# Routing attention and a squared-ReLU FFN on one core: 20 instead of 16 weight blocks rounded in the first half of batch 0, 12 instead of 16 in the second

## The chip, the core and the metric

The kernel runs on one NeuronCore of a Trainium2 chip. The core has five engines, each with its own instruction queue that it works through in order: PE (TensorE, matrix products), DVE (VectorE), ACT (ScalarE), POOL (GpSimd) and SP (SyncE, which here issues DMAs). They run side by side and wait for one another by semaphores. SBUF is the on-chip memory with 128 partitions, PSUM holds the products of PE. The metric is the device time of one execution in microseconds (us); the time before is the median of 15 executions.

## The reference

Inputs: q, k, v of shape (batch 4, heads 8, sequence 768, head width 64), 16 centroids per head, and two weight matrices of 512x2048 and 2048x512, all float32.

```
q_assign = argmax(norm(q) @ norm(centroids).T)          # cluster of each query
k_assign = argmax(norm(k) @ norm(centroids).T)          # cluster of each key
scores   = (q @ k.T) / sqrt(64), -1e9 where the clusters differ
attn     = softmax(scores)
x        = (attn @ v), heads side by side -> (3072, 512)
out      = relu(x @ w_in)**2 @ w_out                    # (3072, 512)
```

## The kernel before

**Units.** The eight heads are taken in four pairs per batch, the 768 queries in two halves of 384, the 768 keys in six chunks of 128. A unit is one pair, one half of the queries and two chunks of keys: three units make a pair's half. Batch 0 has 24 units. Units 0 to 11 are the first half of the queries for pairs 0 to 3, units 12 to 23 the second half; `TWOS`, which is 12, marks the border (L731). Batches 1 to 3 follow pair by pair.

**One unit.** `scores` (L447) makes the products `sc` on PE, in batch 0 a float32 part from `qkT` and a bfloat16 part from `ohT` that sets pairs of different clusters far below the others. ACT takes their exponential (`exp`, L474) into `ex`. Two units later in units 0 to 11, and one or two later from unit 12 on, `times_v` (L505) multiplies by v (`av`). The softmax sums are made in one of two ways: for the first half of batch 0 by PE products with a constant (`sm`, inside `times_v`), otherwise by POOL additions into `acc` (L488, L490) and one short product at the end. `add_up` (L531) takes the reciprocal `r` of the sums on DVE (L545), sends it through DRAM and back over the partitions (`far_r`, `rb`, L548 and L551, by SP), and `finish` (L561) multiplies it into `xT` on DVE (L564). PSUM has two buffers for scores (`ps_sc`), two for `av` and `sm`, and two (`ps_f`) that transposes, logits and FFN products share.

**Preparing the next pair.** In batch 0 the items of `prep` (L416) for the next pair are spread over a pair's three units: three groups of transposes `pt` (L259) with ACT copies into `qkT` (L263), the logits `lg` and their ACT copy `lgs` (L312), the transposes `lt` of these (L322), five DVE steps that find the cluster number, from `mx` (L345) through L346, L349 and L352 to the one-hot rows `oh` (L354), the transposes `po` of `oh` (L389) and two ACT copies into `ohT` (L397, L399). The next pair's scores need `qkT` and `ohT`. From batch 1 on the route goes by DRAM (`words`, `flat`, `qid`).

**The FFN of batch 0** is made in small steps between the units from unit 12 on (`ffn`, L573: products `ph`, then `po` at L591). It starts when `xT` of pair 3's first half is there. The other batches' FFNs run at the end, after all attention, in a form with seven products in place of eight (`ffn_pair`, L604).

**The weights.** The two matrices are cut into 32 blocks of 128 x 512, sixteen of `w_in` and then sixteen of `w_out`, here called blocks 0 to 31. They reach SBUF as 64-bit words, so a block's load is 128 x 1024 32-bit words (512 KB), into one of four buffers (`wstage`, `AHEAD` = 4). `round_weights` (L141) turns a block into the form that the products use: two ACT steps (L150, L152), three DVE steps (L155, L159, L163) and one POOL step (L167). Then `load_weights` issues the load of the fourth next block on SP (L139), which waits until POOL has ended with the block whose buffer it takes.

**What sets the order.** A planner in the framework orders the instructions of each engine from the program's order, the priorities (`tc.high_priority`) and explicit constraints (`tc.issue_after`). The rounding steps of a unit may come only after the last `exp` that was written before them:

```
rounding += 4
while rounding >= 3:
    rounding -= 3
    i = next(to_round, None)
    if i is not None:
        with tc.issue_after(last_exp[0]):
            round_weights(i)
```

Four is added per unit and three taken per block, so the units take 1, 1, 2, 1, 1, 2, ... blocks, and unit 23 takes the last.

Of the kernel before, what the change touches and what calls it, by code (L numbers as in the profile page):

```python
# [25 lines left out]
def kernel(  # L26
# [88 lines left out]
    def load_v(pair):  # L115
        b, hp = divmod(pair, HP)
        raw_v[pair] = loads_v.tile([P, 2, NCH, D], F32, name="v_raw")
        nc.sync.dma_start(
            raw_v[pair], v[b, 2 * hp : 2 * hp + 2].rearrange("h (p j) d -> p h j d", p=P)
        )  # L120
# [16 lines left out]
    def load_weights(i):  # L137
        raw_w[i] = wstage.tile([P, NW, 2], U32, name="w_raw")
        nc.sync.dma_start(raw_w[i], weights[i][1])  # L139
# [134 lines left out]
    def split_words(pair, which):  # L274
        if which == 0:
            words[pair] = dram.tile([2 * NCH, P, 2, 2 * D], U16, name="words")
        flat = loads.tile([P, NCH, 2, 2 * D], U16, name="flat", tag="qk")
        src = raw[pair][which].bitcast(U16).rearrange("p c (d two) -> p c two d", two=2)
        half = NCH // 2
        with tc.issue_after(last_exp[0]):  # L280
            for cols in (slice(0, half), slice(half, NCH)):
                nc.scalar.copy(out=flat[:, cols], in_=src[:, cols])
        nc.sync.dma_start(
            words[pair][NCH * which : NCH * (which + 1)].rearrange("c p two d -> p c two d"),
            flat,
        )
        if which == 1:
            raw.pop(pair)
            load_qk(pair + 1)
# [126 lines left out]
    def prep(pair):  # L416
        if pair < HP:
            return [
                lambda: turn(pair, 0), lambda: turn(pair, 1), lambda: turn(pair, 2),
                lambda: logits(pair), lambda: route(pair),  # L420
                lambda: turn_onehot(pair, 0), lambda: turn_onehot(pair, 1),
            ]

        split = [lambda i=i: split_words(pair + 1, i) for i in range(2 if pair + 1 < NG else 0)]
        first, second = split or (None, None)
        return [
            lambda: turn_words(pair), None, None, first, None, None,
            lambda: logits(pair), None, lambda: route(pair), second, None, None,
            None, None, lambda: spread(pair),
        ]  # L430
# [10 lines left out]
    def first_half(pair, h):  # L441
        return pair < HP and h == 0
# [62 lines left out]
    def times_v(pair, h, c):  # L505
        if c == 0:
            av[pair, h] = ps_av.tile([P, TB], F32, name="av", tag="av")
            if first_half(pair, h):
                sums[pair, h] = ps_av.tile([P, TB // 2], F32, name="sm", tag="av")
        t = ex.pop((pair, h, c))  # L510
        products = [
            dict(
                out=av[pair, h][D * e : D * (e + 1)], lhsT=raw_v[pair][:, e, c + i],
                rhs=t[:, 2 * i + e], start=(c + i == 0), stop=(c + i == NCH - 1),
            )
            for i in range(2) for e in range(2)
        ]
        if first_half(pair, h):
            for i in range(2):
                one = [  # L520
                    ones_products(
                        sums[pair, h], e, t[:, 2 * i + e], c + i == 0, c + i == NCH - 1
                    )
                    for e in range(2)
                ]
                products += [p for both in zip(*one) for p in both]
        together(products, 4000)
# [3 lines left out]
    def add_up(pair, h):  # L531


        b, hp = divmod(pair, HP)
        if first_half(pair, h):
            sm = sums.pop((pair, h))
            nc.scalar.copy(out=xT_of(b, h)[:, hp], in_=av.pop((pair, h)))
        else:
            total = acc.pop((pair, h))
            sm = bank("sm", [P, TB // 2])  # L540
            one = [ones_products(sm, e, total[:, e], True, True) for e in range(2)]
            together([p for both in zip(*one) for p in both])
        row = 4 * (2 * pair + h)
        r = once.tile([P, TB // 2], F32, name="r")
        nc.vector.reciprocal(out=r, in_=sm)  # L545
        r = r.rearrange("(r p) n -> r p n", r=4)[:, 0]
        far = dram.tile([2, TB], F32, name="far_r")
        nc.sync.dma_start(far.rearrange("e (g n) -> (e g) n", g=2), r)  # L548
        rb = rbp.tile([P, TB], F32, name="rb")
        for e in range(2):  # L550
            nc.sync.dma_start(rb[D * e : D * (e + 1)], far[e].partition_broadcast(D))  # L551
        nc.sync.dma_start(seen[row : row + 4], r)
        spread_out[pair, h] = rb
# [177 lines left out]
    TWOS = HP * NCH // 2  # L731
# [17 lines left out]
    def behind_first(u, what=last_logits):  # L749
        return tc.issue_after(what[0]) if u == 0 else ExitStack()  # L750

    def next_pair(u):

        pair, h, c = units[u]
        if c == 0 and pair + 1 < NG and h == 0 and (pair + 1) not in qkT:
            if pair + 1 < HP or pair >= HP:
                return pair + 1
        if u == TWOS + 4:
            return HP
        return None  # L760
# [10 lines left out]
    rounding = 0  # L771
# [6 lines left out]
    def ends(halves):  # L778
        for pair, h in halves:
            b, hp = divmod(pair, HP)  # L780

            with tc.high_priority(offset=1000) if (pair, h) == (HP - 1, 0) else ExitStack():
                finish(pair, h)
            if hp == HP - 1 and (b, h) in PLAIN:
                fill.append(ffn(b, h))

    for u in range(len(units) + 3):
        if u < len(units):
            pair, h, c = units[u]
            if (p := next_pair(u)) is not None:  # L790
                ahead.extend(prep(p))
            if u in (TWOS, TWOS + 2):

                split_words(HP, int(u > TWOS))
            if c == 0 and u + 3 < len(units) and units[u + 3][0] not in raw_v:
                load_v(units[u + 3][0])

            with behind_first(u):
                scores(pair, h, c)

        ends(added)
        added.clear()
        if u < TWOS:
            ready = u - 1
        elif u == TWOS or u % 2 or u >= len(units):
            ready = u

        complete, late = late, []
        while v_next < min(ready, len(units)):
            pair, h, c = units[v_next]  # L810
            times_v(pair, h, c)
            v_next += 1
            if c == NCH - 2:
                (late if h and not HP * NCH <= u < len(units) else complete).append((pair, h))
        for pair, h in complete:
            with tc.high_priority(offset=1000) if first_half(pair, h) else ExitStack():
                add_up(pair, h)
            if h == 1:
                for d in (qkT, ids, qid):
                    d.pop(pair)  # L820
            if h == 1 or pair < HP:
                raw_v.pop(pair)
            added.append((pair, h))

        rounding += 4
        while rounding >= 3:
            rounding -= 3
            i = next(to_round, None)
# [3 lines that stand above are left out]
                if (i := next(loaded, None)) is not None:  # L832
                    load_weights(i)
            elif not later:
                early.close()
                for name, bufs in (("xT", 5), ("out", 2)):
                    later[name] = keep.enter_context(
                        tc.tile_pool(name=name + "_late", bufs=bufs, side="right",
                                     reuse_waits="tile")
                    )  # L840
        share = 0
        if u % 2 == 0 or not TWOS < u < len(units):
            n = 2 if TWOS < u < len(units) else 1
            share = max(0, left[0] - RESERVE) * sum(map(density, range(u, u + n)))
            share //= max(1, sum(map(density, range(u, ENDS))))
        goal = left[0] - share

        for i in range(3):
            if i == 2:
                fill_steps(share * 2 // 3)  # L850
            if ahead:
                with behind_first(u, masked if i else last_logits):
                    (ahead.pop(0) or int)()
        fill_steps(left[0] - goal)
# [235 lines left out]
```

## Time and profile before

| | us |
|---|---|
| median of 15 executions | 979.13 (976.9 to 984.9) |
| the profiled execution | 983.98 |
| its span, first to last instruction | 982.2 |
| PE busy | 962.1 (98%) |
| DVE busy | 565.5 (58%) |
| POOL busy | 380.6 (39%) |
| ACT busy | 316.3 (32%) |
| exp of unit 0 starts | 19.11 |
| exp of unit 12 starts | 77.61 |
| FFN products of batch 0 run through from | 88.77 |
| the last FFNs (L670, L701) start | 542.2 |

Times inside the span are counted from its first instruction. "Busy" counts the time in which an instruction of the engine is under way; matrix products are pipelined, so a busy PE need not be a PE at its peak. "x <- y" in a row of waits or in brackets behind an instruction says what ended the idle time before it. The starts of exp in units 1 to 14 are 22.94, 27.59, 33.78, 38.06, 43.64, 49.76, 54.04, 59.63, 65.75, 69.00, 72.26, 77.61, 82.15 and 86.14.

### The profile page before, as it was taken

Reading aid. Unit: us, or ns where it says so; the run is one execution under the profiler, and the core shown is the slowest. Engines: PE = TensorE matmul, PEld = TensorE weight load, DVE = VectorE, ACT = ScalarE, POOL = GpSimd, SP = SyncE. Lnnn points to the kernel's source line nnn. Section 1 sums busy time; section 2 is a strip of 40 time slices with the busy share of each in tenths; the row PEclk is TensorE's granted clock in tenths of the full one; section 3 lists DMA queues with packets and bytes.
Section 4 is the critical chain, followed back from the end, with each engine's and each line's share of the span. In section 5 each row is a group of like instructions: output and inputs, shape, how many; then the busy total and the mean of one; then the engine's idle time right before and its main releaser. Section 6 shows DMA issues by size and latency. Waiting matters only on the chain.

```text
span 982.2 us, 12064 instructions
## 1 busy us (share of the span) xinstructions
PE 962.1 (98%) x4479; PEld 553.2 (56%) x4479; DVE 565.5 (58%) x913; ACT 316.3 (32%) x511; POOL 380.6 (39%) x277
## 2 busy tenths in 40 slices
PE   8999999999999999999999999999999999999997
PEld 5444444443344444444443555888556888556886
DVE  4779766665666656566657865532566531656331
ACT  4787755443435554454331111000111000111000
POOL 1237865556565565555656431002231002231000
PEclk9999999999999999999999999999999999999999
DMA  9657681455544445443310000000000000000000
GB/s 239 193 166 217 192 195 61 111 117 129 133 114 118 121 121 122 113 119 89 88 36 17 20 1 0 12 22 22 11 1 1 22 22 22 1 1 0 22 22 25
DMA packets 127746, 74.54 MB, mean 76 GB/s; under 512 B 90944, under 2 KB 119104, under 8 KB 127680
## 3 DMA queue, kind: packets, MB, share of 16 engines
q1 hardware_dynamic: 125968, 73.26, 28.2%
q8 instruction: 38, 0.62, 0.3%
q10 hardware_dynamic: 1712, 0.43, 0.2%
q14 instruction: 28, 0.23, 0.1%
HBM read 48.27 MB, written 15.86 MB: 65 GB/s over the span
## 4 chain that ended last, share of the span: by engine, by line
PE 85%; issue 5%; POOL 3%; DMA 2%; DVE 2%; SPq 1%; ACT 0%; POOLq 0%; DVEq 0%; ACTq 0%
PE bank L701 22%; PE bank L670 22%; PE po L591 8%; PE ph L578 7%; PE sc L91 6%; PE sc L94 6%; PE av L91 5%; PE av L94 5%; POOL w_in L167 2%; PE sm L91 1%; PE lg L91 1%; DMA rb<-far_r 1%; DMA qid<-far 1%; DVE ex L478 1%; SPq L109 1%
## 5 line engine op out<-in xcount | busy, mean ns | idle before, releaser
L490 POOL TENSOR_TENSOR acc<-acc,ex 128x768 f32<-128x768 f32 x112 | 206.8, 1846 | 109.5 <-DVE ex L478 93.1
L478 DVE SCALAR_TENSOR_TENSOR ex<-qid,ids,sc 128x384 f32<-128x384 bf16 x288 | 157.9, 609 | 65.7 <-ACT sc L474 41.9
L474 ACT ACTIVATE sc<-sc 128x768 f32<-128x768 f32 x144 | 108.5, 793 | 160.5 <-PE sc L94 142.7
L94 PE MATMUL sc<-qkT 64*128 64x384 f32 x576 | 153.6, 507 | 0.5
L94 PE MATMUL av<-ex,v_raw 128*64 128x384 f32 x576 | 136.9, 495 | 0.0
L659 POOL TENSOR_TENSOR w_s<-w_in 128x256 f32<-128x256 f32 x24 | 18.1, 756 | 273.9 <-PE bank L701 162.0
L640 DVE TENSOR_TENSOR g<-bank,g 128x384 f32<-128x384 f32 x144 | 77.8, 555 | 79.1 <-PE bank L670 77.9
L578 PE MATMUL ph<-xT,w_in 128*128 128x384 f32 x256 | 91.8, 499 | 4.8 <-DVE best L346 2.2
L701 PE MATMUL bank<-w_out,g 128*128 128x256 f32 x432 | 95.2, 379 | 0.0
L591 PE MATMUL po<-w_out,gT 128*128 128x512 f32 x192 | 91.7, 609 | 0.0
L91 PE MATMUL sc<-qkT 64*128 64x384 f32 x192 | 88.0, 539 | 3.2 <-DVE ex L478 3.2
L701 PEld LDWEIGHTS bank<-w_out,g 128*128 128x128 f32 x432 | 82.1, 190 | 11.8
L640 DVE TENSOR_TENSOR osb<-bank,osb 128x256 f32<-128x256 f32 x54 | 22.1, 423 | 107.6 <-PE bank L701 102.2
L94 PEld LDWEIGHTS sc<-qkT 64*128 64x128 f32 x576 | 65.5, 187 | 28.0 <-issue 5.7
L91 PE MATMUL av<-ex,v_raw 128*64 128x384 f32 x192 | 81.1, 504 | 0.0
L488 POOL TENSOR_TENSOR acc<-ex 128x768 f32<-128x768 f32 x28 | 51.5, 1840 | 52.4 <-DVE ex L478 42.3
L578 PEld LDWEIGHTS ph<-xT,w_in 128*128 128x128 f32 x256 | 45.7, 189 | 43.8 <-issue 14.1
L670 PE MATMUL bank<-xT,w_in 128*128 128x384 f32 x192 | 69.9, 487 | 0.0
L670 PE MATMUL bank<-x_t,w_s 128*128 128x384 f32 x192 | 69.8, 486 | 0.0
L670 PE MATMUL bank<-xT,w_s 128*128 128x384 f32 x192 | 69.8, 486 | 0.0
L94 PEld LDWEIGHTS av<-ex,v_raw 128*64 128x64 f32 x576 | 49.7, 137 | 34.7 <-issue 34.4
L701 PE MATMUL bank<-w_t,g 128*128 128x256 f32 x288 | 65.1, 379 | 0.0
(127 smaller groups left out, 1228.3 us busy)
## 6 DMA issues: line engine op xcount, KB each, us to landing
words<-flat SPq DMA_DIRECT2D x24, 384.0 KB
w_raw<-in_moe_w_in_dram SPq DMA_DIRECT2D x16, 512.0 KB
w_raw<-in_moe_w_out_dram SPq DMA_DIRECT2D x16, 512.0 KB
v_raw<-in_v_dram SPq DMA_DIRECT2D x20, 384.0 KB
rb<-far_r SPq DMA_DIRECT2D x64, 96.0 KB
q_raw<-in_q_dram SPq DMA_DIRECT2D x31, 192.0 KB
k_raw<-in_k_dram SPq DMA_DIRECT2D x31, 192.0 KB
out_dram<-osb SPq DMA_DIRECT2D x23, 256.0 KB
```

The lines of the kernel that those rows point to most:

```text
L91: last = nc.tensor.matmul(**next(products))
L94: last = nc.tensor.matmul(**product)
L167: nc.gpsimd.tensor_tensor(out=dst, in0=dst, in1=lo, op=ALU.add)
L474: last_exp[0] = nc.scalar.activation(out=t[:, 2 * i : 2 * i + 2] if pair < HP else src, in_=src, func=ACT.Exp, scale=SCALE).ins
L478: last_mask[0] = nc.vector.scalar_tensor_tensor(out=t[:, 2 * i + e], in0=qid[pair][1][:, h, e], scalar=ids[pair][:, ch % NB, 2 + ch // NB, ...
L488: nc.gpsimd.tensor_tensor(out=acc[pair, h], in0=t[:, 0:2], in1=t[:, 2:4], op=ALU.add)
L490: nc.gpsimd.tensor_tensor(out=acc[pair, h], in0=acc[pair, h], in1=t[:, 2 * i : 2 * i + 2], op=ALU.add)
L578: nc.tensor.matmul(ph, lhsT=w_in[:, kk, f * P : (f + 1) * P], rhs=xT[b, h][:, kk], start=(kk == 0), stop=(kk == KT - 1),)
L591: nc.tensor.matmul(po, lhsT=gT[f][:, i * P : (i + 1) * P], rhs=w_out[:, f], start=(f == 0), stop=(f == FT - 1),)
L640: nc.vector.tensor_tensor(out=out, in0=bank, in1=to, op=ALU.add)
L670: nc.tensor.matmul(bank, lhsT=operands[j][0][:, kk], rhs=operands[j][1][:, kk], start=(kk == 0), stop=(kk == H2 - 1),)
L701: nc.tensor.matmul(bank, lhsT=operands[j][0][:, f], rhs=operands[j][1][:, f], start=(f == 0), stop=(f == F2 - 1),)
```

## The change

Per unit five is added in units 0 to 11 and three in units 12 to 23, in place of four in both; three are taken per block as before.

```diff
-        rounding += 4
+        rounding += 5 if u < TWOS else 3
         while rounding >= 3:
             rounding -= 3
             i = next(to_round, None)
```

Units 0 to 11 now take 1, 2, 2, 1, 2, 2, ... blocks, 20 in all: all of `w_in` and four blocks of `w_out`. Units 12 to 23 take one each. The steps of a block, its buffers and the number of blocks stay as they are; as a block's load is issued behind the rounding of the fourth block before it, the loads move with the rounding. The planner then orders a few other instructions differently in units 1 to 8: the transposes `lt` stand behind all eight float32 score products of their unit in place of four (in unit 2 also behind three of the four mask products), and in unit 3 the scores stand ahead of `po` and `av` behind it.

## The prediction

> **What bounds the kernel now.** I read the page's engine lines first, then the stages, then PE's waits in each stage, then the timelines of the chains that PE waits for.
>
> ```profile
> PE 962.1 (98%) x4479; PEld 553.2 (56%) x4479; DVE 565.5 (58%) x913; ACT 316.3 (32%) x511; POOL 380.6 (39%) x277
> ```
>
> PE is busy 98% of the span, so the time is PE's work plus what PE waits. The stage view divides it (start:end, length, then busy us and count for PE, PE's weight loads, DVE, ACT, POOL; then clock, DMA share, GB/s):
>
> ```profile
> 31.95:85.40 53.45, 53.04 (x456) 25.51 (x454) 41.24 (x60) 44.46 (x71) 21.20 (x16) 1.00 0.62 193
> 85.40:180.00 94.60, 88.19 (x416) 42.09 (x415) 68.33 (x70) 56.81 (x97) 66.39 (x39) 0.98 0.57 154
> ```
>
> The first row is units 3 to 14 of scores, the second the rest of batch 0 with the FFN's first products. In the first PE idles 0.4 us and ACT works 44.5 of 53.5: what is added must fit the gaps of ACT and DVE. In the second PE idles 6.4 us, and its waits from 84 to 180 us are (who waits <- for whom: us, times, longest):
>
> ```profile
> PE ph L578 <- DVE best L346: 2.2, 1, 2.2
> PE sc L91 <- DVE ex L478: 1.5, 1, 1.5
> PE ph L578 <- DVE r L545: 1.4, 1, 1.4
> PE ph L578 <- DVE xT L564: 1.2, 1, 1.2
> ```
>
> All four wait for DVE, whose queue holds rounding steps ahead of the awaited one. Now the first half closely, the timeline around unit 8 (start, duration, engine, instruction, [idle before <- releaser]):
>
> ```profile
> 56.85 0.71 ACT L152 ACTIVATE w_raw<-w_raw 128x512 f32<-128x512 uint32 x1
> 57.43 0.49 ACT L312 COPY lgs<-lg 128x384 f32<-128x384 f32 x1
> ...
> 57.97 0.55 PE L322 MATMUL lt<-ident,lgs 128*128 128x128 f32 x3 [0.21 <-ACT lgs L312]
> 58.79 0.43 DVE L163 TENSOR_SCALAR w_in<-w_raw 128x512 uint32<-128x512 uint32 x1
> 59.13 0.55 DVE L345 TENSOR_REDUCE mx<-lt 128x24 f32<-128x384 f32 x1
> ...
> 61.62 0.56 DVE L354 TENSOR_TENSOR oh<-best,ids 128x384 bf16<-128x384 bf16 x1
> ...
> 63.15 0.84 PE L389 MATMUL po<-ident_b,oh 128*128 128x128 bf16 x12
> ...
> 65.87 1.41 POOL L167 TENSOR_TENSOR w_in<-w_in,w_raw 128x512 int32<-128x512 int32 x1 [5.29 <-DVE w_in L163]
> 66.17 1.39 DVE L163 TENSOR_SCALAR w_in<-w_raw 128x512 uint32<-128x512 uint32 x1
> ```
>
> This is the chain that finds the next pair's clusters: lgs (ACT), lt (PE), mx to oh (DVE), po (PE). oh ends at 62.18 and PE, busy with av and sm until then, takes po at 63.15: the chain has 0.97 us of slack. The last rows show L163 at 1.39 us beside POOL's L167, where alone it is 0.43.
>
> **The change, part by part.** 32 blocks before and after, the last still in unit 23. Units 0-11 round 20 instead of 16, units 12-23 round 12 instead of 16. A block is two ACT steps (1.20 us from one block's start to the next's, 61.02 to 62.22), three on DVE (0.70 + 0.43 + 0.43), one on POOL (1.30) and a 512 KB load on SP. The two programs' instruction lists show where the extra block goes: in units 1, 4 and 7 ahead of lgs on ACT (in 4 and 7 with all its DVE steps ahead of mx), in unit 10 ahead of unit 11's exp.
>
> *Third pair (units 6-8), from T = 49.76, unit 6's exp.* lgs started at T+7.67; one block later is T+8.87, it ends at 9.36, lt starts at 9.41. PE, which now has all eight score products ahead of lt, is free at T+7.09+1.40 = 8.49 and waits 0.92; after lt 0.48 and the mask products 0.42 the scores end at T+10.31 (before 59.62, T+9.86). DVE cannot begin the second block before its L152 ends at T+8.99. Then L155 0.73, the first block's L163 0.43, L159 0.46, and L163 at 1.39, because POOL's L167 of the first block has just begun: T+12.0. mx 0.57, L346 0.59, L349 0.72, L352 0.59, L354 0.56: oh at T+15.03. PE is through av (1.44) and sm (2.09) at T+13.84 and waits 1.2. Before, po began at T+13.39: the pair loses 1.7. With L163 at 0.43 oh comes at 14.07 and 0.7 is lost; if lt's wait alone counted, 0.4; with L349 at the 1.30 that it took at 28.07 beside L167, 2.3. I take 1.7, since L163 took 1.39 or 1.40 in the first half wherever two blocks stand together.
>
> *Second pair.* The same 1.7, and an inheritance: the first pair changes the order (scores of unit 3 ahead of po, av behind it), so that PE reaches unit 4's scores 1.03 + 1.82 after unit 3's exp starts, when ACT still has 1.39 + 1.17 + 1.08 to do. That exp is 0.8 late, and with it the last copy ahead of the logits and lgs: 2.4 (0.4 to 3.0). *First pair.* lgs moves from 25.45 to 26.65; between lt and oh now stand the second block's L163, slowed by L167 to 1.05, a third block's L155 and L159, and L349 slowed to 1.15: oh at 34.1 instead of 30.55. PE has unit 3's scores (1.40) to do meanwhile, is free at 32.9 and waits 1.2; with lt's wait 1.6 (0.3 to 1.6).
>
> *Units 9-11.* A unit of 3.26 us (69.00 to 72.26) must hold exp 1.39, two blocks 2.40 and an xT copy 0.36: unit 11's exp is 0.9 late, hidden by PE's av and sm (3.53). Block 19's load waits for POOL's block 15: issued at 71.82, by the trace's landings down at 77.20 (5.4; the other blocks' loads took 3.5 to 7.1). ACT wants it at 73.15 + 1.39 + 1.20 = 75.7, on the old clock. Behind it on ACT are the two flat copies and unit 12's exp, 2.4 late, which PE's av of units 10 and 11 (2.7) covers; on DVE L155 and then r of pair 3, that begins r, far_r, rb, xT, for which the FFN waits (88.77). On SP block 22's load, waiting for POOL's block 18, now stands between far_r and rb. The FFN is late by 0 to 1.5; I take 1.0.
> [...]
>
> First half: 1.6 + 2.4 + 1.7 + 1.0 = **+6.7** (1.1 to 8.4). The four earlier blocks' POOL steps (5.2) fit its idle 32 us, and the loads' 2 MB add 39 GB/s to 193. On SP they stand ahead of far_r and rb of pairs 0-2, which only the FFN needs.
>
> *Units 12-23,* one block per unit instead of 1, 1, 2. (a) r at 103.70 stood behind four blocks begun since 88.5, two of them unit 14's; with one fewer, DVE is there when sm ends (101.0): 1.4. (b) mx at 128.50 stood behind two blocks, which stay; but L155, L159 and L163 took 1.60, 1.94 and 1.90 beside POOL's acc adds, which would end some 2 us sooner: 1.2 of 2.2. (c) ex at 168.12 stood behind unit 23's second block, now gone: 1.4. The wait for xT stays. Together **-4.0** (0 to -5.1). What is late next is (b)'s remainder, then the row qid at 227 us on the chain of waits, which does not change. The rest of the four blocks' work is worth nothing: PE's FFN products cover it.
>
> Net +2.7. On the profiled execution (983.98, span 982.2 plus 1.8 around it) that is 986.7; this execution is 4.85 above the median of 979.13, so for the median I say **981.8**.
>
> **The rivals.** (1) *Faster:* the chain's slack holds. L163 runs at 0.43 and the loads land in 3.7 us; the pairs lose 0.3 + 0.7 + 0.7, the last term is 0, the second half pays 4.0: -2.3, 976.8. For it: such landings exist (67.30 to 71.07). Against: the two 1.39s. It decides where po waits under 0.5 us. (2) *Nothing is paid back:* POOL's acc adds (1.85 each) slow DVE as before, and the three waits stay: +6.7, 985.8. (3) *The faster rate isn't reached.* From ACT's start on a block to the landing of the fourth next took 8.2 to 12.8 us; the tightest spacing will be 11.05 (35.17, unit 3's block, to 46.22, unit 5's second). If ACT waits for loads in each pair and holds exp 0.7 us: +2.1 more, 983.9.
>
> **How the numbers follow.** A measurement of this kernel tells about 0.2% (2 us) from no change. Forecast 0.50 (0.36 of it slower, 0.14 same; own range 979.3 to 985.5), rival 1 0.25 (0.16 faster, 0.09 same), rival 2 0.15, rival 3 0.10 (both slower): slower 0.61, same 0.23, faster 0.16. The bounds give 1.1 - 5.1 = -4.0 to +8.4; rival 1 sets the low end and rival 2 with its spread the high one: 976.5 to 987.0.
>
> **What would show it.** In units 5 and 8, lt after about 0.9 us of idle for lgs and po over 1 us late for oh; unit 12's exp near 84, not 77.6; L150 of block 19 waiting for its load; no PE wait for r near 105 nor for ex near 170. I am wrong if po starts without a wait, or the FFN restarts less than 4 us after 88.8.

## The result, and the profile after

The changed kernel takes 982.42 us (median of 12 executions, 981.11 to 987.78) against 978.84 for the kernel before in the same comparison: a ratio of **1.0042, 95% interval 1.0030 to 1.0055**. It is slower, by about 4 us. 981.8 had been forecast.

The profiled execution has a span of 980.7 us (982.57 with what lies around it), less than the 982.2 shown of before. That is no contradiction: the profiled execution of before lost 4.1 us at the very start, ahead of unit 1's exp (22.94 us there, 18.81 here). All comparisons of the two traces below are therefore counted from unit 1's exp. So counted, the changed kernel ends 2.64 us later.

The page's engine line, and then the stage view (start:end, length, busy us and count of PE, PE's weight loads, DVE, ACT, POOL; clock, DMA share, GB/s) over the stretches that answer to the two rows of before (the second reaches 2.0 us further into the program than its counterpart):

```profile
PE 956.7 (98%) x4479; PEld 551.0 (56%) x4479; DVE 556.9 (57%) x913; ACT 315.9 (32%) x511; POOL 379.7 (39%) x277
```

```profile
29.95:87.27 57.32, 52.22 (x448) 24.90 (x448) 46.53 (x69) 47.42 (x77) 24.80 (x18) 1.00 0.67 201
87.27:180.90 93.63, 89.69 (x421) 43.29 (x423) 54.06 (x62) 52.43 (x90) 62.31 (x37) 0.98 0.54 142
```

The two stages have traded places. Units 3 to 14 took 53.45 us with PE idle for 0.4; they now take 57.32 with 5.1 idle. The stretch behind them had 6.4 idle in 94.60 us; up to the same point of the program (178.93) it now takes 91.66 with 3.9 idle. PE's waits from 15 to 200 us of the changed kernel (who waits <- for whom: us, times, longest) name them:

```profile
PE ph L578 <- DVE xT L564: 3.0, 1, 3.0
PE lt L322 <- ACT lgs L312: 2.7, 3, 1.3
PE po L389 <- DVE oh L354: 2.3, 3, 1.0
PE sc L91 <- ACT ex L474: 1.5, 1, 1.5
PE ph L578 <- DVE best L346: 0.9, 1, 0.9
```

In the same stretch of the kernel before, the waits for lgs came to 1.0 (the row below), those for oh to nothing, and those for best, ex, r and xT stood at 2.2, 1.5, 1.4 and 1.2, as shown with the prediction.

```profile
PE lt L322 <- ACT lgs L312: 1.0, 3, 0.6
```

So the rows for lgs, oh, xT and the exp of unit 12 are up by 1.7 + 2.3 + 1.8 + 1.5 = 7.3 us, and the rows for best, r and ex at 168 us are down by 1.3 + 1.4 + 1.5 = 4.2. How much later each unit's exp starts than before shows the same build-up and pay-back (counted from unit 1's exp, us):

| unit 3 | 6 | 9 | 12 | 14 | FFN restart | 18 | 20 | 25 | 27 | end |
|---|---|---|---|---|---|---|---|---|---|---|
| 2.13 | 2.78 | 4.23 | 7.68 | 6.00 | 7.70 | 7.87 | 4.99 | 3.47 | 3.06 | 2.64 |

The FFN restart is the ph product that waits for pair 3's xT. In both traces PE's granted clock is 0.50 for one stretch of 3.41 us ahead of the last 10 us; in the changed kernel it lies behind the FFN restart, in the kernel before at 130.3 us, so the steps next to these two places contain it with opposite signs and the end does not.

The timeline of the changed kernel around the second pair's preparation in unit 5 (start, duration, engine, instruction, [idle before <- releaser]):

```profile
40.33 0.55 PE L322 MATMUL lt<-ident,lgs 128*128 128x128 f32 x3 [0.69 <-ACT lgs L312]
40.56 0.42 DVE L163 TENSOR_SCALAR w_in<-w_raw 128x512 uint32<-128x512 uint32 x1
41.06 1.41 POOL L167 TENSOR_TENSOR w_in<-w_in,w_raw 128x512 int32<-128x512 int32 x1 [3.61 <-DVE w_in L163]
41.35 1.41 DVE L163 TENSOR_SCALAR w_in<-w_raw 128x512 uint32<-128x512 uint32 x1
42.69 0.54 DVE L345 TENSOR_REDUCE mx<-lt 128x24 f32<-128x384 f32 x1
...
45.20 0.56 DVE L354 TENSOR_TENSOR oh<-best,ids 128x384 bf16<-128x384 bf16 x1
45.81 0.84 PE L389 MATMUL po<-ident_b,oh 128*128 128x128 bf16 x12 [0.97 <-DVE oh L354]
```

The second block's L163 begins 0.29 us after POOL's L167 of the first block, ends 0.29 us after it and takes 1.41 us, where the first block's took 0.42. mx waits for it, oh comes 1 us late, and PE has nothing left. In unit 8 lt waits 0.71 and po 0.97, in unit 2 1.35 and 0.30.

And the timeline of the changed kernel around units 11 to 14, where the lateness grew from 4.23 to 7.70:

```profile
75.37 0.71 ACT L150 ACTIVATE w_out<-w_raw 128x512 f32<-128x512 f32 x1 [0.72 <-DMA w_raw<-in_moe_w_out_dram]
77.25 1.39 DVE L163 TENSOR_SCALAR w_out<-w_raw 128x512 uint32<-128x512 uint32 x1
78.48 0.72 ACT L150 ACTIVATE w_out<-w_raw 128x512 f32<-128x512 f32 x1 [1.82 <-DMA w_raw<-in_moe_w_out_dram]
79.28 1.42 DVE L159 TENSOR_SCALAR w_raw<-w_out 128x512 f32<-128x512 f32 x1
...
81.15 1.49 ACT L474 ACTIVATE ex<-sc 128x768 f32<-128x768 f32 x2
81.22 1.34 DVE L545 RECIPROCAL r<-sm 128x192 f32<-128x192 f32 x1
81.99 0.59 PE L91 MATMUL sc<-qkT 64*128 64x384 f32 x1 [1.50 <-ACT ex L474]
82.59 0.52 SPq L548 DMA_DIRECT2D far_r<-r  x1
85.60 1.13 SPq L551 DMA_DIRECT2D rb<-far_r  x2
90.11 2.07 DVE L564 SCALAR_TENSOR_TENSOR xT<-xT,rb 128x384 f32<-128x384 f32 x1 [1.48 <-ACT w_out L150]
92.33 3.36 PE L578 MATMUL ph<-xT,w_in 128*128 128x384 f32 x6 [3.01 <-DVE xT L564]
```

ACT stands still for the loads of blocks 18 and 19 (0.72 and 1.82), and the exp of unit 12 behind them holds PE for 1.50. Pair 3's sums were ready at 75.95, but r starts only at 81.22, behind rounding steps on DVE, two of which took 1.39 and 1.42. From there the chain r, far_r, rb, xT runs to the FFN. (The bracket at xT names an ACT step that happened to end at the same moment; the second of the rb transfers had landed at 89.99.)

### The profile page after: what moved, and what is told of

Its sections match the earlier page's. It is cut to its first block, busy times and chain, and to the rows that moved or that the text cites. A ratio compares the mean times of both kernels' runs of the same rounds, so it can differ in the third digit from the quotient of the medians.

```text
span 980.7 us, 12066 instructions
## 1 busy us (share of the span) xinstructions
PE 956.7 (98%) x4479; PEld 551.0 (56%) x4479; DVE 556.9 (57%) x913; ACT 315.9 (32%) x511; POOL 379.7 (39%) x277
## 4 chain that ended last, share of the span: by engine, by line
PE 87%; issue 4%; POOL 3%; DMA 2%; DVE 1%; ACT 1%; SPq 1%; POOLq 0%; DVEq 0%; ACTq 0%
PE bank L701 22%; PE bank L670 22%; PE ph L578 8%; PE po L591 8%; PE sc L91 7%; PE sc L94 6%; PE av L91 6%; PE av L94 5%; POOL w_in L167 2%; PE sm L91 1%; PE lg L91 1%; SPq L109 1%; DMA w_raw<-in_moe_w_out_dram 1%; ACT ex L474 1%; DMA w_raw<-in_moe_w_in_dram 1%
## 5 line engine op out<-in xcount | busy, mean ns | idle before, releaser
L94 PE MATMUL sc<-qkT 64*128 64x384 f32 x576 | 150.5, 502 | 0.5
L91 PE MATMUL sc<-qkT 64*128 64x384 f32 x192 | 87.2, 534 | 2.7 <-ACT ex L474 1.5
```

The costliest lines, as they stand in the source:

```text
L91: last = nc.tensor.matmul(**next(products))
L94: last = nc.tensor.matmul(**product)
```

## The experiments

All runs stand beside runs of the kernel before on the same chip; ratios are to these, with their 95% intervals. Where line numbers of an experiment are shifted by its edit, its rows are quoted as they are.

**1 and 2: the change in one half of batch 0 at a time.**

```diff
-        rounding += 5 if u < TWOS else 3
+        rounding += 5 if u < TWOS else 4     # experiment 1
```

> Units 0-11 as in the changed kernel (five in three units), units 12-20 with four in three units as before (1, 1, 2 blocks), none after. My theory (the cost lies in the first half, the second half's thinner rounding pays part of it back): the FFN restarts about 7.5 us later than before, counted from unit 1's exp, as in the changed kernel; PE's waits for r (1.4, unit 15-17) and for mx/best (2.2) are there again, the one for ex at unit 25 (1.4) is not, as no block is left then. 7.5 - 1.4 = +6 us against before, ratio 1.006. Rival (nothing is paid back, the first half alone is the difference): the same time as the changed kernel, +3.6 to +4.1, ratio 1.004.

985.05 us, 1.0075 (1.0054 to 1.0096): slower by 7.3 us.

```diff
-        rounding += 5 if u < TWOS else 3     # experiment 2
+        rounding += 4 if u < TWOS else 3
-    to_round = iter(range(len(weights)))
-    loaded = iter(range(len(weights)))
+    to_round = iter(range(28))
+    loaded = iter(range(28))
+    nc.gpsimd.memset(w_out[:, 12:16], 0.0)
```

> Units 0-11 with four in three units as before, units 12-23 with one block each as in the changed kernel: 28 blocks. The last four blocks are left out (neither loaded nor rounded, their part of w_out is set to zero by one POOL fill at the start), so the output lacks their part. My theory: FFN restart as before (88.8 less the start's difference), the waits for r, best and ex fall from 1.4 + 2.2 + 1.5 to about 1 in all: -4 us, ratio 0.996. Rival (nothing is paid back): within 1 us of before, ratio 0.999 to 1.001.

973.81 us, 0.9958 (0.9940 to 0.9976): faster by 4.1 us.

The two runs have the signs of the prediction's halves (+6.7 and -4.0), and their sum, +3.2, agrees with the whole change's +4.1 within their intervals of about 2 us each. But experiment 1 is not the first half alone. At the old pace its last block is rounded in unit 20, so the waits for best (0.9) and for ex (none) fell there too, by 2.8 us together. Against that, PE waited 2.95 for r of the next pair's half, at 106.96 us, where the kernel before waited 1.45 and the changed kernel not at all, and behind this wait the clock stood at half for 6.83 us in place of 3.41. That its 7.3 lies near 6.7 is therefore in part luck. Its FFN restart was 4.52 us late, not 7.5 as expected, with the very same first half: block 19's load held ACT for 0.59 in that execution and for 1.82 in the changed kernel's, unit 12's exp held PE not at all, and PE waited 1.1 for xT in place of 3.0. The term of units 9 to 13 thus differs by some 3 us between two runs that share the first half.

In experiment 2's profile the waits for r, best and ex came to 0.2, 0.9 and nothing, 1.1 in all where about 1 had been expected. The wait for xT, 1.2 before, which the prediction left standing, was gone as well. The run leaves out the last four blocks altogether, their loads included.

**3: the same pace, but the units with two blocks are others.**

```diff
-    rounding = 0
+    rounding = 1
```

Units 0, 2, 3, 5, 6, 8, ... take two blocks, and units 1, 4 and 7, behind which lgs comes, take one.

> The changed kernel with the counter started at 1, so that units take 2, 1, 2, ... blocks instead of 1, 2, 2, ...; same 20 and 12. The extra block of a pair now stands in units 0, 3, 6 (beside the qkT copies) instead of 1, 4, 7 (ahead of lgs). My theory (the place of the block matters: lgs and the route's DVE steps behind it): PE's waits for lgs fall from 2.7 to about 1, those for oh from 2.3 to 0, the load wait of block 19 stays: about 4 us less than the changed kernel, ratio to before 0.999 to 1.001. Rival (ACT's and DVE's occupancy matters: four blocks more, wherever they stand): as the changed kernel, ratio 1.004.

977.73 us, 0.9988 (0.9976 to 1.0001). PE's waits from 15 to 200 us of this kernel:

```profile
PE ph L578 <- DVE xT L564: 2.4, 1, 2.4
PE lg L91 <- ACT qkT L263: 1.3, 1, 1.3
PE lt L322 <- ACT lgs L312: 1.0, 3, 0.6
...
PE po L389 <- DVE oh L354: 0.3, 1, 0.3
```

lgs is back at the 1.0 of before and oh at 0.3. The waits for lgs and oh come from where the second block stands, not from five blocks in three units. The order is not free, though: lg now waits 1.3 for a copy ahead of unit 1's exp, which is itself 1.1 later for it, and the wait for xT stays at 2.4. Counted from unit 0's exp, the FFN restart is 4.0 us late, against 7.7 in the changed kernel. With the whole computation it is the fastest version here, by one part in a thousand against the kernel before, which its interval does not quite separate from no change.

**4: block 19 a unit later.**

```diff
-        rounding += 5 if u < TWOS else 3
+        rounding += {11: 2, 12: 6}.get(u, 5 if u < TWOS else 3)
```

> The changed kernel with block 19 rounded in unit 12 (which then has two blocks, 19 and 20) instead of unit 11; everything else as there, 19 blocks in units 0-11. My theory (block 19's load comes late, holds unit 12's exp and pair 3's r): PE's wait of unit 13's scores for ex (1.5) goes, the wait for xT falls from 3.0 to about 1.2, the waits for lgs and oh stay: 3 us less than the changed kernel, ratio 1.001. Rival (the load wait is hidden anyway, or unit 13's exp is held instead): less than 1 us less, ratio 1.003 to 1.004.

984.11 us, 1.0053 (1.0032 to 1.0074): a miss. The wait of 1.5 for unit 12's exp was gone, as expected, but PE waited 3.75 for xT in place of 3.0. DVE had no more work then:

```profile
90.87 0.56 DVE L564 SCALAR_TENSOR_TENSOR xT<-xT,rb 128x384 f32<-128x384 f32 x1 [5.40 <-DMA rb<-far_r]
```

DVE stood idle for 5.40 us for rb, and rb was issued late because far_r, 3 KB, had taken 4.13 us from issue to landing. So taking away block 19's wait does not by itself bring the FFN restart forward. It does not show that this wait is without effect: r stood 4.16 us behind the sums in place of 5.27, but the same edit put block 22's load 0.43 us ahead of far_r, which then took 1.2 us longer.

**5: POOL's step cut short.** For blocks 0 to 19 the low halves of the weights are added on 64 of 512 columns, in float32 in place of int32.

```diff
-            out=dst, in0=hi, scalar1=3, scalar2=None, op0=ALU.logical_shift_left
+            out=dst, in0=hi, scalar1=0 if i < 20 else 3, scalar2=None, op0=ALU.logical_shift_left
-        dst, lo = dst.bitcast(I32), lo.bitcast(I32)
+        kind, n = (F32, 64) if i < 20 else (I32, NW)
+        dst, lo = dst.bitcast(kind)[:, 0:n], lo.bitcast(kind)[:, 0:n]
```

> The changed kernel, but for blocks 0 to 19 POOL's add of L167 covers 64 of the 512 columns and the shift of L163 is by 0 (the low halves of the products' weights are left wrong, so the output is not the reference's). This tells the price of DVE's steps slowed beside POOL: L163 took 1.39 us beside L167 and 0.43 alone. Theory: with L167 short, L163 runs at about 0.43 in units 2, 5 and 8, PE's wait for oh (2.3 us in the changed kernel) falls below 0.8, its wait for lgs stays at 2.7, r of pair 3 starts up to 2 us sooner; the buffers also come free 1.1 us sooner. Ratio to the kernel before 0.999 to 1.001. Rival: oh is late for the number of DVE steps ahead of it, not for their slowness: the wait for oh stays over 1.5 and the ratio at 1.003 to 1.004.

974.72 us, 0.9964 (0.9946 to 0.9981). PE's waits, and the timeline of unit 5:

```profile
PE lt L323 <- ACT lgs L313: 2.7, 3, 1.3
PE ph L579 <- DVE best L347: 0.9, 1, 0.9
...
```

```profile
40.25 0.43 POOL L168 TENSOR_TENSOR w_in<-w_in,w_raw 128x64 f32<-128x64 f32 x1 [4.59 <-DVE w_in L163]
40.54 0.43 DVE L163 TENSOR_SCALAR w_in<-w_raw 128x512 uint32<-128x512 uint32 x1
...
43.24 0.56 DVE L355 TENSOR_TENSOR oh<-best,ids 128x384 bf16<-128x384 bf16 x1
43.96 0.84 PE L390 MATMUL po<-ident_b,oh 128*128 128x128 bf16 x12
```

L163 takes 0.43, po starts without a wait, and the waits for oh, for unit 12's exp and for xT are all gone; that for lgs, made on ACT, is unchanged at 2.7. The FFN restart is 0.43 us late in place of 7.70. Of the first half's loss, the rise of lgs from 1.0 to 2.7 is the extra block on ACT; the rest hangs on POOL's step.

**6: the preparation written ahead of the rounding.** In each unit the code that rounds stands behind the code that prepares the next pair and places the FFN's steps (the two parts of the loop trade places, nothing else is changed).

```diff
+        for i in range(3):                  # items of prep, moved up
+            ...
         rounding += 5 if u < TWOS else 3
         ...
-        for i in range(3):
-            ...
```

> The changed kernel with the rounding of each unit written behind the preparation of the next pair, so that lgs stands ahead of the second block on ACT in units 1, 4 and 7 and the routing steps (mx to oh) ahead of part of the second block's steps on DVE. The number of blocks per unit is the changed kernel's. Theory: PE's waits for lgs and oh in these units (2.7 and 2.3 us) come from the second block standing ahead of them and fall to about 1.0 and 0.5; the blocks then end later, which moves the exps of units 3, 6 and 9 by under 1 us, and the terms of units 9 to 13 stay. Ratio 1.000 to 1.002. Rival: ACT and DVE have too little room in these units in whatever order, the exps are as late as lgs was: 1.004.

981.81 us, 1.0039 (1.0022 to 1.0057). PE's waits:

```profile
PE po L389 <- DVE oh L354: 3.9, 3, 1.9
PE ph L578 <- DVE xT L564: 2.8, 1, 2.8
PE sc L91 <- ACT ex L474: 1.7, 2, 1.1
...
PE lt L322 <- ACT lgs L312: 0.6, 3, 0.2
```

The rival had the time right. lgs fell from 2.7 to 0.6 as the theory said, and oh rose from 2.3 to 3.9 with a new second wait for exp: what ACT gave, DVE took back.

**7: two loads behind rb**, in experiment 4's kernel.

```diff
-                    load_weights(i)
+                    held.append(i)
+                    while held and not (held[0] in HOLD and not rb_out):    # HOLD = (21, 22)
+                        j = held.pop(0)
+                        with tc.issue_after(rb_out[0]) if j in HOLD else ExitStack():
+                            load_weights(j)
...
+        if (pair, h) == (HP - 1, 0):          # in add_up, behind rb's DMAs
+            rb_out.append(out.ins)
```

> The kernel of the fourth experiment (block 19 rounded in unit 12), and the loads of blocks 21 and 22 are issued after rb of pair 3 instead of ahead of far_r. There far_r took 4.13 us from issue to landing behind these loads (1.61 in the kernel before, with no load in flight ahead of it but one), and PE waited 3.8 for xT. Theory: with the loads behind it far_r lands in 1.6 to 2.0, xT comes 2 us sooner, PE's wait for xT falls to about 1.5 and the ratio from 1.0053 to about 1.003. Rival: xT is late because r is late (it started at 80.2, in the kernel before at 77.6), and far_r's landing is spread of the run: the wait stays over 3 and the ratio at 1.005.

981.36 us, 1.0047 (1.0031 to 1.0063), against 1.0053 in experiment 4: no difference that can be told. The mechanism came as the theory said: far_r landed in 1.60 us, xT started at 87.57 in place of 90.87, and no wait for xT is left. In its place stands the first of these rows among PE's waits; the second is from ACT's timeline:

```profile
PE ph L581 <- ACT gT L588: 2.7, 1, 2.7
```

```profile
88.75 0.68 ACT L150 ACTIVATE w_out<-w_raw 128x512 f32<-128x512 f32 x1 [3.77 <-DMA w_raw<-in_moe_w_out_dram]
```

ACT now stands 3.77 us before the held-back load, and behind it wait the copies gT that the FFN needs. The FFN is held by one thing or the other at the same place.

**8: experiments 3 and 6 together.** To experiment 6's kernel is added:

```diff
-    rounding = 0
+    rounding = 1
```

> The kernel of the third experiment (five blocks in three units in the order 2, 1, 2, so that the units in which a pair is prepared get one) with the rounding written behind the preparation as in e6. Theory: what was left there of waits for lgs, lg and oh (1.0, 1.3 and 0.3 us) goes down by about half: ratio 0.9965 to 0.998, ahead of both kernels. Rival: nothing is left to win there, since the units with two blocks have no preparation: 0.999 as in the third experiment.

977.56 us, 0.9996 (0.9984 to 1.0009): the rival; nothing is won over experiment 3. The waits for lg and oh are gone and that for lgs fell to 0.6, but PE waited 1.7 for an exp and 1.0 for r, as it had not in experiment 3.

**9: experiment 5's edit in the kernel before.** To experiment 5's kernel is added:

```diff
-        rounding += 5 if u < TWOS else 3
+        rounding += 4
```

> The kernel before with the edit of the fifth experiment (for blocks 0 to 19 POOL's add covers 64 columns and L163 shifts by 0; the output is not the reference's). It is the control of that experiment: both paces without L163 slowed beside L167. Theory: the change's loss in the first half is made by the slowed steps, its gain in the second half is not, so without them five-then-three is faster than four by 2 to 4 us: this kernel at 0.9985 to 1.0005, against 0.9964 for the changed one. Rival: the edit speeds up both paces alike, by some 7 us: this kernel at 0.992 to 0.994.

974.87 us, 0.9973 (0.9951 to 0.9994): between theory and rival. POOL's short step takes 2.6 us off the old pace and 7.6 off the new one. With POOL's full step the new pace costs 0.42%; with the short one it stands at 0.9964 against 0.9973, a difference of -0.0009, and the two intervals together (the root of 0.0018 and 0.0021 squared and added) leave about 0.003 to either side: no loss can be seen. In FFN restarts: 7.70 late with the full step; with the short one, 0.43 for the new pace and -0.71 for the old.

**10 and 11: two other distributions**, both from experiment 3's order.

```diff
-    rounding = 0
+    rounding = 1
-        rounding += 5 if u < TWOS else 3
+        rounding += 5 if u < 9 else 4 if u < 14 else 3      # experiment 10
+        rounding += 5 if u < 9 else 4 if u < TWOS else 3    # experiment 11
```

> The changed kernel in the order 2, 1, 2 as in the third experiment in units 0 to 8 (15 blocks), then four in three units as in the kernel before up to unit 13, then one in each unit: blocks 18 and 19 are a unit or more later, so that DVE has fewer steps ahead of r of pair 3. Theory: PE's wait for xT (2.4 us in the third experiment) falls to the 1.2 of the kernel before and the waits near 105 and 170 us stay away: ratio 0.9965 to 0.9985. Rival: the blocks moved behind unit 11 meet r at 104 us as in the kernel before (1.4 us): 0.9985 to 1.0.

> The tenth experiment's kernel with one block in each unit from unit 12 on, so that unit 13 has one block instead of two and the last block is rounded in unit 24. Theory: ahead of the tenth by the wait for r, where there is one: 0.996 to 0.998. Rival: the block in unit 24 brings back the wait for ex at 168 us (1.5), and the two are equal.

980.18 us, 1.0016 (0.9999 to 1.0034), and 979.32 us, 1.0012 (0.9996 to 1.0028): both misses, not better than experiment 3. PE waited 3.3 and 2.0 for xT, where 1.2 had been expected. The chain from the end of pair 3's sums to xT, read out of eight traces, tells why (us):

| kernel | sums' end to r's start | far_r, issue to landing | sums' end to xT's start |
|---|---|---|---|
| before | 1.77 | 1.61 | 10.6 |
| changed | 5.27 | 2.95 | 14.2 |
| experiment 3 | 3.24 | 2.80 | 12.5 |
| 4 | 4.16 | 4.13 | 14.8 |
| 5 | 1.65 | 3.99 | 10.5 |
| 7 | 4.30 | 1.60 | 11.5 |
| 10 | 4.23 | 3.85 | 14.3 |
| 11 | 3.21 | 4.45 | 13.1 |

Moving blocks moved neither of the two terms back: r still stood behind rounding steps on DVE for 3.2 to 4.2 us, and far_r landed late. These are single executions, and the chain varies: in experiment 1, with the changed kernel's first half, the three columns are 3.55, 3.10 and 12.05.

**12: the shift in another form.** POOL's step is left whole.

```diff
-        nc.vector.tensor_scalar(
-            out=dst, in0=hi, scalar1=3, scalar2=None, op0=ALU.logical_shift_left
-        )
+        nc.vector.scalar_tensor_tensor(
+            out=dst, in0=hi, scalar=3, in1=none.to_broadcast([P, NW]),
+            op0=ALU.logical_shift_left, op1=ALU.bitwise_or,
+        )
```

> The changed kernel with L163's shift written as a scalar_tensor_tensor (shift, then bitwise or with a column of zeros), so that POOL's add keeps its 512 columns and its place and the output is the reference's. L155, of the same operation, took 0.68 to 0.70 us in the first half also where L167 ran beside it. Theory: it is the slowing of L163 beside L167, not the length of L167 or the number of steps, that made oh late: L163 now takes 0.7 everywhere, in each of the three pairs DVE loses 0.3 on the first L163 and gains 0.7 on the second, PE's wait for oh falls from 2.3 us to under 1.2, r of pair 3 starts 0.5 to 1 us sooner. Ratio 1.000 to 1.0025. Rival: the new form is slowed beside L167 as well, or the gain and the loss cancel over the blocks: waits as in the changed kernel, 1.0035 to 1.005.

986.96 us, 1.0076 (1.0061 to 1.0090): a miss, further than the rival. Two rows of PE's waits and the timeline of unit 5:

```profile
PE po L392 <- DVE oh L357: 6.4, 3, 3.1
PE lt L325 <- ACT lgs L315: 2.7, 3, 1.3
```

```profile
41.94 0.69 DVE L163 SCALAR_TENSOR_TENSOR w_in<-w_raw,none 128x512 uint32<-128x512 uint32 x1
42.71 1.43 POOL L168 TENSOR_TENSOR w_in<-w_in,w_raw 128x512 int32<-128x512 int32 x1 [4.32 <-DVE w_in L163]
43.36 1.34 DVE L163 SCALAR_TENSOR_TENSOR w_in<-w_raw,none 128x512 uint32<-128x512 uint32 x1
...
47.58 0.55 DVE L357 TENSOR_TENSOR oh<-best,ids 128x384 bf16<-128x384 bf16 x1
48.19 1.46 PE L392 MATMUL po<-ident_b,oh 128*128 128x128 bf16 x12 [3.10 <-DVE oh L357]
```

The new form is longer beside POOL too: the second L163 begins inside POOL's step, ends 0.56 us after it and takes 1.34 us, where the first took 0.69. My premise, taken from L155, was wrong: the rows of L155 at 0.68 beside L167 had begun a moment ahead of it or 0.02 us ahead of its end, and the two that began well inside it between 20 and 80 us of the changed kernel took 1.57. What the run does show is how little room there is: each block takes 0.26 us more of DVE, in units 5 and 8 L352 (L349 of the other kernels) now meets POOL's next step and takes 1.28 and 1.31 in place of 0.72, and the wait for oh rises from 2.3 to 6.4.

Experiment 5 shortens POOL's step itself, which also frees each buffer some 1 us sooner, and experiment 12 was meant to take these two apart. It does not, so how much of the 7.3 us at the FFN restart is longer DVE steps and how much earlier loads stays open.

## Why the prediction was right, and where its sum was off

The direction and the mechanism were right: 981.8 forecast, 982.42 measured, in the forecast case (a first half that loses, a second that gives part of it back). That the time was met so closely is in part luck: the pairs lost 1.4 us less than forecast and units 9 to 11 with what follows 2.3 more, and the latter term was 3 us smaller in experiment 1's execution.

| step | predicted, us | measured, us |
|---|---|---|
| first pair: lt for lgs, po for oh | 1.6 | 0.75 + 0.30 (+ 0.3 before pt) |
| second pair | 2.4 | about 0.5 + 0.97 |
| third pair | 1.7 | about 0.5 + 0.97 |
| units 9 to 11 and what follows | 1.0 (0 to 1.5) | 3.3 |
| first half | 6.7 | 7.3 in PE's waits, 7.70 at the FFN restart, 7.3 in experiment 1's time (not the first half alone), 4.52 at its FFN restart |
| (a) r at 105 | -1.4 | -1.4 |
| (b) best at 128 | -1.2 | -1.3 |
| (c) ex at 168 | -1.4 | -1.5 |
| second half | -4.0 | -4.2 in PE's waits, -4.1 in experiment 2's time (there with xT's 1.2) |

(The measured waits for lgs are 1.35, 0.69 and 0.71 less 0.6, 0.2 and 0.2 of before.)

*The pairs* lose by the predicted chain at three quarters of the size, 4.3 in place of 5.7 with the 0.3 before pt. lt waited 0.69 and 0.71 where 0.9 was foretold, and po 0.97 in both where it was over 1. L163 took 1.41 in each, as assumed. The term that failed is the second pair's inheritance: unit 4's exp was not later than unit 3's (2.13 us late in unit 3, 1.33 in unit 4), so nothing was handed on.

*Units 9 to 11* is the mis-sized step, outside its own bounds. Two things were wrong in it. I had PE's av products cover the lateness of unit 12's exp; it came 3.4 us after its scores, not 2.4, because block 18's load was late as well as block 19's, and PE waited 1.50. And I had r behind "L155" alone. It stood 5.27 us behind DVE steps, against 1.77 before, two of them at 1.39 and 1.42 beside POOL's step; far_r then took 2.95 to land in place of 1.61. The prediction put the load of block 22 between far_r and rb. It does stand there, but rb went out at 85.60, 0.06 us behind far_r's landing: it waited for that and not for the load. Two loads moved from ahead of far_r to behind rb went with a landing in 1.60 us in place of 4.13 (experiment 7 against 4).

*The second half* came out term by term in size. For (b) the reason held in part only: POOL's add still stood beside the block ahead of mx, L155 and L159 took 1.77 and 1.92, and L163 alone, behind the add's end, ran at 0.43 in place of 1.90. Experiment 1 shows a wait for r near 105 us of 2.95 in place of 1.45 behind the same first half, so the lower pace may remove more there than the 1.4 that I booked; one execution does not settle that.

*The signs.* On its own clock the changed kernel restarts the FFN at 92.33, only 3.5 us after 88.8, where the prediction called less than 4 a sign of being wrong. That compares two clocks whose starts differ by 4.1 us; counted from unit 1's exp the restart is 7.70 late. Unit 12's exp, so counted, is 7.68 late, at 85.3 on the clock of before, where near 84 was named. The waits for r near 105 and for ex near 170 are gone, and ACT waited for block 19, as forecast.

*The rivals.* Rival 1 (the chain's slack holds, with L163 at 0.43) is the case that experiment 5 comes near: with POOL's step short, the waits for oh are gone. Its gain of 2.3 us is not shown: against its own control, experiment 9, the new pace is ahead by 0.9 us, give or take some 3. Its deciding point, po waiting under 0.5 us, was met in the first pair only. Rival 2 (nothing is paid back) is refuted by experiment 2 and by the waits gone in the changed kernel. Rival 3 (ACT waits for loads in each pair) happened at one place in units 9 to 12, and there its cost went into the term of units 9 to 11.

Block 19's load, issued at 72.43, had 5.4 us in the prediction and the loads of rival 1 had 3.7; ACT began on it 6.0 us after its issue and had waited 1.82 for it.

## What to carry to other kernels

When work is moved into a stretch where PE idles 0.4 of 53 us, ask of each added step not how long it takes but what it stands ahead of, and price the DVE steps that will meet POOL by the end of POOL's step, not by their own length: here L163 and L159, begun inside L167, ended 0.28 or 0.29 us after it, at up to 1.42 us in place of 0.43. The same number of added blocks made the FFN restart 4.0 us late in one order (2, 1 and 2), which the second half paid back, and 7.7 us late in the other (1, 2 and 2), where the whole cost 4 us. A wait that is taken away at a junction of two chains, as xT for gT in experiment 7, is only worth the distance to the other chain: compute that first.

## What the runs showed of the hardware that was not expected

**Rounding steps of DVE that began inside POOL's step ended after it.** Between 20 and 80 us of the changed kernel every L163 and L159 that began while POOL's L167 was under way ended 0.28 or 0.29 us after it (eight of eight, lasting 1.05 to 1.42, where alone they took 0.43), and two such L155 0.55 after it (1.57 each; a third began 0.02 us ahead of its end and kept 0.69). A rounding step (L155 or L159) that began just ahead of L167 kept its length, and L167 behind it took 1.40 to 1.69 in place of 1.30. L345 and L346, which read lt from PSUM, kept their 0.54 to 0.56 inside L167. The new L163 of experiment 12 ended 0.56 us after POOL's step, much as L155 did. What in a step decides how it fares beside L167 was not taken apart.

**Most long waits of PE had a stretch of slower clock behind them.** The stage view of the changed kernel behind the FFN's wait of 3.01 us, with the granted clock third from the end:

```profile
88.00:93.20 5.20, 2.19 (x8) 1.07 (x7) 3.72 (x3) 2.65 (x5) 4.76 (x4) 1.00 0.97 310
93.20:96.60 3.40, 3.40 (x7) 1.75 (x6) 3.30 (x5) 1.02 (x2) 1.85 (x2) 0.50 0.53 116
96.60:100.00 3.40, 3.40 (x13) 1.83 (x13) 2.67 (x2) 1.02 (x2) 3.32 (x3) 1.00 0.46 104
```

For 3.41 us the clock is at half; half of that, about 1.7 us, is my estimate of what it costs beside the wait itself. The 16 ph products behind this wait took 7.09 us; behind experiment 3's wait of 2.40, with no such stretch, they took 5.40. Over all 14 traces, PE waited 2 us or more in one piece 12 times between 15 and 200 us, and 9 of these had such a stretch that began near the wait's end (6.83 us long after experiment 1's 2.95 and experiment 12's 3.10); behind 2.40, 3.29 and 2.52 in experiments 3, 10 and 12 there was none. Of the 29 waits of 1.0 to 2.0 us two were followed by one: 1.45 in experiment 9 and 1.74 in experiment 8. Of all these, the shortest wait with such a stretch behind it was 1.45 us long, the longest without one 3.29. Whether one execution has such stretches seems to vary: experiment 10's profile had none here, and the mean granted clocks of its 12 executions went from 1.000 down to 0.992, their times from 976.36 to 982.31. That the two belong together was not tested by itself.

**A 3 KB transfer behind large ones.** far_r landed 1.60 or 1.61 us after its issue in the kernel before and in experiment 7, where the last 512 KB load had been issued 2.9 or more us ahead of it, and 2.95 in the changed kernel and 4.13 in experiment 4, where one had been issued 2.2 and 0.4 us ahead. Experiment 7's edit against experiment 4 moves the loads of blocks 21 and 22 alone. The weight loads are not all, though: the 384 KB transfer of `words` goes out on the same queue, and with it 0.55 us ahead far_r took 2.32 in experiment 9, though the last weight load was 3.8 us back, and 3.99 in experiment 5. Which of them counts for how much was not taken apart.
